# Attention with a routed mixture of experts: the late routing and scatters of batch 5 stand behind head pair 28, and GpSimd drains its DMA queue once ahead of the last 256 rows

## The chip, the cores and the metric

The kernel runs on one core of a Trainium2 chip. The metric is the device time of one execution in microseconds (us); of several runs the median counts. One execution was recorded by the hardware profiler, and all rows below are from that one. The engines are TensorE (PE), VectorE (DVE), ScalarE (ACT), GpSimd (POOL) and SyncE (SP); transfers are issued by an engine's queue and carried by 16 DMA engines.

## The reference

Eight batches of eight heads, 576 positions, head size 64. Attention with rotated q and k, and behind it a mixture of eight experts in which each of the 4,608 tokens goes to the one expert with the largest logit. Cut to what matters:

```python
def _attn_ref(q, k, v):                       # (8, 8, 576, 64)
    q_rot, k_rot = rotate(q), rotate(k)
    scores = scale * q_rot @ k_rot.T
    attn = exp(scores - max) / sum
    return attn @ v

x = attn_out.transpose(0, 2, 1, 3).reshape(4608, 512)

def _moe_ref(x, modality_id, w_gate, modality_bias, w1, w2):
    logits = x @ w_gate + modality_bias[modality_id]      # 8 experts
    e_idx = np.argmax(logits, axis=1)
    gate_w = softmax(logits)[arange(N), e_idx]
    for e in range(8):
        mask = e_idx == e
        h = np.maximum(x[mask] @ w1[e], 0.0)              # 512 -> 1024
        out[mask] = gate_w[mask, None] * (h @ w2[e])      # 1024 -> 512
    return out
```

## The kernel before, in words

The attention works through 32 pairs of heads, n = 0 to 31; four pairs make one batch, so batch 4 ends with pair 19, batch 5 with pair 23, batch 6 with pair 27. For a pair the rope (lines 461 to 469 on POOL) rotates q and k in `ST` and splits them into a high and a low part `HL`; ACT makes the high part at line 452, and a swap (line 477, four transfers on SP's queue) writes `SW`, which is `HL` with its halves exchanged. PE forms the scores (line 492) from `HL` and `SW`, DVE takes the extremes (line 501), ACT the exponentials (line 510), PE turns them round (line 515) and multiplies with v (line 573). DVE and ACT copy between these steps (lines 548 and 452).

When a batch's last pair is done, its rows go to a table `X` in DRAM (lines 633 and 635, SP's queue), and the batch is routed in fifteen steps, `RK0` to `RK14`: logits and their maximum on DVE, the one-hot rows on POOL (`RK6`, lines 687 to 689), the ranks of the tokens within their expert on PE (`RK8`, lines 701 and 703, into a half of a PSUM tile), the running counts `RUN` on DVE (`RK9`, lines 709 and 710), a guard on ACT (`RK10`), the token's own rank on POOL (`RK11`, line 718), the gate on DVE (`RK12`, line 721, into `VAL`), the row number on DVE (`RK13`, line 724) and its cast to a whole number on POOL (`RK14`, line 728). `VO` then writes `VAL` (token id and gate) into the last two columns of `X` (lines 640 and 641). `BKj` loads the j-th 128 tokens of the batch from `X` into one of two buffers `XL`, which alternate in the order of the calls (lines 756 and, for the last 64 tokens, 758), and `SCj` scatters them with an indirect transfer on POOL's queue into the expert's part of a table `XS` (line 738).

The mixture begins while the attention still runs: a first plan uses the rows of batches 0 to 4 in `XS`. A block reads rows of `XS` (lines 1007 and 1030), DVE transposes them, PE multiplies with the first and the second weights (lines 1084, 1202 and 1103, 1326), and POOL scatters the finished rows to the output (line 1114). The weights come in by transfers of SP (line 1034). Behind the blocks of 512 rows a function `chain` does the last planned 256 rows (two stores, line 1114) and a block of 128 rows (two stores, line 1427). A branch for further blocks follows, which is not taken with these inputs (line 1647).

All of this is in an order written out by hand. Each step is put in a list with a key, `EDGE[n].get(name, KEYS[name]) + PER * n` with `PER` = 14.438, and the list is sorted by it. PE, ACT, DVE, POOL and SP each carry out their instructions in that order. `EDGE[19]` are thus the exceptions for the steps of batch 4, `EDGE[23]` those of batch 5. Behind the list the blocks of the mixture are called one after the other.

Of the kernel before, what the change touches and what calls it, by code (L numbers as in the profile page):

```python
# [19 lines left out]
B, H, S, D = 8, 8, 576, 64  # L20
# [110 lines left out]
        "LD1": -42.214,  # L131
    },
    19: {
    },
    23: {
    },
    25: {
        "RE": 11.575, "F2": 13.246, "A_F2": 14.351, "B_F2": 14.486, "RI": 16.427, "AVB": 18.725, "OTB": 20.519, "OUT": 26.426,
# [92 lines left out]
def tile_attention_moe(ctx: ExitStack, tc: tile.TileContext, qk, v, mod, wg, mb, w1, w2, rope, cf, ci, out):  # L231
    nc = tc.nc
# [405 lines left out]
    def vout(b, eng=nc.sync):  # L638
        xd = X[b * S:(b + 1) * S, DM:XU]
        eng.dma_start(out=xd[0:512, :].rearrange("(p j) w -> p j w", j=4), in_=VAL[:, b, 0:4, :].bitcast(F32))  # L640
        eng.dma_start(out=xd[512:576, :], in_=VAL[0:64, b, 4, :].bitcast(F32))
# [93 lines left out]
    def scatter(b, j):  # L735
        oi = bt_[b]["oi"]
        n = P if j < 4 else 64
        inst = nc.gpsimd.indirect_dma_start(  # L738
            out=XS, out_offset=bass.IndirectOffsetOnAxis(ap=oi[0:n, j:j + 1], axis=0),
            in_=xl[b, j][0:n], in_offset=None, bounds_check=E * RS - 1, oob_is_err=False).ins  # L740

        for _b, x in placed:
            tc.declare_no_dep(inst, x, reason="rows of other tokens")
        placed.append((b, inst))
        if b >= NPL:
            for x in taken:
                tc.declare_no_dep(inst, x, reason="the first plan's blocks lie before the rows of later batches")
# [4 lines left out]
    def back(b, j, eng=nc.sync):  # L752
        t = xl[b, j] = XL[len(xl) % 2]
        xd = X[b * S:(b + 1) * S, 0:XU]
        if j < 4:
            eng.dma_start(out=t[:, 0:XU], in_=xd[0:512, :].rearrange("(p j) w -> j p w", j=4)[j])
        else:
            eng.dma_start(out=t[0:64, 0:XU], in_=xd[512:576, :])

    def pads():  # L760
        nc.vector.tensor_copy(CNT, RUN[0:1, B, :])
        for e in range(E):
            r = nc.sync.value_load(CNT[0:1, e:e + 1], min_val=0, max_val=E * RS - BLK)
            inst = nc.sync.dma_start(out=XS[bass.ds(r, BLK), 0:XU], in_=ZR[:, :]).ins
            for _b, x in placed:
                tc.declare_no_dep(inst, x, reason="rows behind those of the tokens")
            for x in taken:
                tc.declare_no_dep(inst, x, reason="the first plan's blocks are full")
            placed.append((B, inst))
# [224 lines left out]
    def m_plan(s):  # L994
        ph, i = slots[s]
        pl = PLB if ph else PLA
        ms[s] = dict(
            e=nc.sync.value_load(pl[0:1, 0, i:i + 1], min_val=0, max_val=E - 1),
            r=nc.sync.value_load(pl[0:1, 1, i:i + 1], min_val=0, max_val=E * RS),
            c=nc.sync.value_load(pl[0:1, 2, i:i + 1], min_val=0, max_val=1))  # L1000

    def m_ix(s):
        d = ms[s]
        k = nt[s]
        ix = d["ix"] = ixp.tile([P, 4, 2], I32, name="ix", tag="ix")
        tab = XS[bass.ds(d["r"], k * P), DM:XU].rearrange("(q a g) w -> g q a w", a=k, g=4)
        m_taken(s, nc.sync.dma_start(out=ix[:, 0:k, :].bitcast(F32), in_=tab).ins)
# [12 lines left out]
    def m_rows(s, j=0):  # L1020
        d = ms[s]
        n = 4 * nt[s]
        if n == 4:
            ho = d["ho"] = ixp.tile([P, 2], I32, name="ho", tag="ho", bufs=1)
            for h in range(2):
                nc.gpsimd.tensor_scalar(ho[:, h:h + 1], d["ix"][:, 0, 0:1], 2.0, float(h), op0=ALU.mult, op1=ALU.add)
        rows = XS[bass.ds(d["r"], nt[s] * P), 0:DM].rearrange("(q r) (i f) -> i q r f", r=n, i=4)[:, :, 8 * j:8 * j + min(n, 8)]
        x = rows_of(s, j).rearrange("p t g f -> p (t g) f")[:, 0:min(n, 8)]
        for i in range(4):
            m_taken(s, nc.sync.dma_start(out=x[32 * i:32 * i + 32], in_=rows[i]).ins)  # L1030
# [26 lines left out]
    def m_split(i, g):  # L1057
        m_hi(i, g)
        m_lo(i, g)

    def m_tr(s, t, j=0):
        x = rows_of(s, j)[:, t]
        nc.vector.transpose(x, x)

    def m_tre(s, t, part=None):
        x = rows_of(s)[:, t].rearrange("p g (c q) -> p c g q", q=32)
        oh, ol = (a[:, :, t * P:(t + 1) * P].rearrange("p c (g q) -> p c g q", q=32) for a in (XTH, XTL))
        if part != 1:
            acopy(oh, x)
        if part != 0:  # L1070
            sub(ol, x, oh.bitcast(F32))
# [390 lines left out]
    def J(k_, nm, n, f, *a):  # L1462
        jobs.append((k_ + PER * n, len(jobs), f, a))
# [30 lines left out]
    for n in range(NPAIR):  # L1494
        def K_(nm, f, *a):
            J(EDGE.get(n, {}).get(nm, KEYS[nm]), nm, n, f, *a)

        for u in range(9):
            K_(f"S{u}", scores, n, u)
            K_(f"MN{u}", rowmin, n, u)  # L1500
            K_(f"EX{u}", expo, n, u)
        for f in ("F0", "F1", "F2", "F3", "FA", "FB"):
            K_(f, fill, n, f)
            for g in range(2):
                K_(f"{'AB'[g]}_{f}", evac, n, f, g)
        for w in range(2):
            c = "AB"[w]
            K_(f"AV{c}", AV, n, w)
            K_(f"OT{c}", avout, n, w)
            K_(f"EV{c}", ev, n, 1 - w)  # L1510
        K_("OUT", outp, n)
        for w in range(2):
            K_("R" + "EI"[w], rsum, n, w)
        if n > 0:
            for part, nm in ((1, "T1"), (0, "T2"), (2, "R"), (3, "HI"), (4, "LO")):
                K_(nm, rope_, n, part)
            for i in range(2):
                K_("SW" + "HL"[i], swap, n, i)
        K_("LV", loadv, n)
        if n > 2:  # L1520
            K_("LD1", load, n, 1)
            K_("LD", load, n, 0)
        if n % 4 == 3:
            K_("BIAS", bias, n // 4)
            K_("XO", xout, n // 4)
            steps = [(f,) for f in route(n // 4)]
            scats = [(scatter, n // 4, j) for j in range(5)]
            if n == z:

                planned = plan()  # L1530
                steps[0:2] = [(each, lambda f: f(), *steps[0:2])]
                late = steps + [(lambda: [vout(B - 1, nc.gpsimd)] + [(back(B - 1, j, nc.gpsimd), scatter(B - 1, j)) for j in range(5)] + [pads()],)] + [(each, next) + ((planned, None),) * 4] * 13
                continue
            for i, x in enumerate(steps):
                K_(f"RK{i}", *x)
            eng = nc.sync if n // 4 < B - 2 else nc.gpsimd
            K_("VO", vout, n // 4, eng)
            for i, x in enumerate(scats):
                K_(f"BK{i}", back, n // 4, i, eng)
                K_(f"SC{i}", *x)  # L1540
# [49 lines left out]
    def chain(lo, hi, begun):  # L1590
        if not begun:
            for g in range(4):
                m_split(0, g)
            for t in range(2):
                m_tr(lo, t)
                m_tre(lo, t)
        for s in range(lo, hi):
            nxt = s + 1 < hi
            half = nt[s] == 1
            if nxt:  # L1600
                if s + 2 < hi:
                    m_rows(s + 2)
                if s + 3 < hi:
                    m_plan(s + 3)
                    m_ix(s + 3)
                for g in range(4):
                    m_load1(s + 1, g)
            if half:
                m_half(s)
            else:  # L1610
                for g in range(4):
                    m_split(1, g)
                    m_l1(s, g)
                    m_l1e(s, g)
            if nxt:
                for g in range(2):
                    m_split(0, g)
                for t in halves(s + 1):
                    m_tr(s + 1, t)
                for t in halves(s + 1):  # L1620
                    m_tre(s + 1, t)
                for g in range(4):
                    m_load2(s + 1, g)
            last = nxt and nt[s + 1] == 1
            if not half:
                m_l2(s, 0)
            if last:
                for g in (2, 3):
                    m_split(0, g)
            if not half:  # L1630
                m_l2(s, 1)
            if nxt and not last:
                for g in (2, 3):
                    m_split(0, g)
# [6 lines left out]
    for s in range(2, NA + NSB):  # L1641
        m_super(s, s + 1)
    assert not late and next(planned, 0) == 0
    chain(NA + NSB, ns, True)
    order.close()
    tot = nc.values_load(TOT[0:1, 0:1], min_val=0, max_val=NB_MAX)
# [103 lines left out]
```

## Time and profile before

| | us |
|---|---|
| median of three runs | 882.19 |
| the three runs | 881.38, 882.19, 886.98 |
| the profiled execution, whole | 884.29 |
| its span on the core | 882.5 |
| busy in it: PE, DVE, ACT, POOL | 833.9, 708.9, 612.2, 453.5 |

The granted TensorE clock was 0.99 of full speed on the mean. The span is the time from the first to the last record of the core; the profiled execution took 1.8 us more than it. A timeline row gives start, duration, engine, line, operation and the names written and read; in brackets stands how long the engine was idle before and what ended that. An engine name with a q behind it (POOLq, SPq) is the engine's sequencer, which carries out semaphores, drains and DMA issues.

### The profile page before, as it was taken

How to read it: one execution, taken by the hardware profiler on the slowest of the kernel's cores; microseconds unless marked ns; L12 is line 12 of the kernel's file. 1: busy time of each engine (PE TensorE's matmuls, PEld its weight loads, DVE VectorE, ACT ScalarE, POOL GpSimd, SP SyncE). 2: the span in 40 equal slices, each digit the busy share in tenths (PEclk: the TensorE clock that was granted, in tenths of full speed). 3: DMA queues.
4: the chain of work that ended last, by engine and by line, in shares of the span. 5: the costliest groups of instructions: out<-in, count | busy, mean ns of one | idle time of the engine just before them, and what ended most of it. 6: DMA issues, size and time to landing. Idle time of an engine off the chain costs nothing.

```text
span 882.5 us, 24889 instructions
## 1 busy us (share of the span) xinstructions
PE 833.9 (94%) x9528; PEld 688.7 (78%) x9528; DVE 708.9 (80%) x1595; ACT 612.2 (69%) x1311; POOL 453.5 (51%) x365
## 2 busy tenths in 40 slices
PE   2899999999999999888999999999999999999992
PEld 2677777777777777676778989898989898989882
DVE  6888898888898888777888577989898998979360
ACT  2898989889888888777975446464656474748360
POOL 2999979989899898999511211024201112020100
PEclk9999999999999999999999999999999999999996
DMA  8877868979788797875877961377955413530520
GB/s 262 229 231 193 260 169 259 265 211 283 205 262 245 215 279 205 249 213 171 251 213 187 328 181 49 60 219 224 282 139 186 114 38 88 169 101 8 186 73 14
DMA packets 116330, 165.80 MB, mean 188 GB/s; under 512 B 31180, under 2 KB 76894, under 8 KB 116204
## 3 DMA queue, kind: packets, MB, share of 16 engines
q1 hardware_dynamic: 107468, 139.18, 55.2%
q0 software_dynamic: 7392, 23.34, 7.5%
q8 instruction: 77, 1.26, 0.6%
q10 hardware_dynamic: 1344, 1.62, 0.6%
q14 instruction: 49, 0.40, 0.1%
HBM read 118.14 MB, written 34.70 MB: 173 GB/s over the span
## 4 chain that ended last, share of the span: by engine, by line
PE 79%; DMA 5%; POOL 4%; ACT 4%; DVE 3%; issue 2%; SPq 1%; ACTq 0%; POOLq 0%; DVEq 0%
PE psY L1326 20%; PE ps L573 15%; PE psH L1202 14%; PE ps L492 13%; PE ps L515 9%; PE ps L608 2%; DMA SW<-HL 2%; PE psY L1202 2%; ACT P L510 1%; PE psH L1084 1%; PE psY L1103 1%; DMA ST<-in_rope_dram 1%; POOL HL L469 1%; DVE sc L501 1%; DMA ST<-in_moe_w_dram 1%
## 5 line engine op out<-in xcount | busy, mean ns | idle before, releaser
L501 DVE CUSTOM_DVE_ANT_1 sc<-ps,ZERO 128x576 f32<-128x576 f32 x288 | 206.6, 748 | 24.0 <-PE ps L492 11.3
L510 ACT ACTIVATE P<-sc,mn 128x576 f32<-128x576 f32 x256 | 195.5, 767 | 5.9 <-DVE mn L501 4.7
L492 PE MATMUL ps<-HL 64*128 64x288 f32 x960 | 167.9, 309 | 13.7 <-ACT HL L452 10.8
L492 PE MATMUL ps<-SW 64*128 64x288 f32 x960 | 168.1, 309 | 7.6 <-DMA SW<-HL 7.5
L1114 POOL DMA_INDIRECT out_dram<-sc,ix x36 | 43.4, 1206 | 222.1 <-ACT sc L1113 215.4
L492 PEld LDWEIGHTS ps<-HL 64*128 64x128 f32 x960 | 134.4, 188 | 19.5 <-ACT HL L452 10.8
L492 PEld LDWEIGHTS ps<-SW 64*128 64x128 f32 x960 | 134.3, 188 | 11.9 <-issue 9.4
L573 PE MATMUL ps<-PH,AT 128*64 128x320 f32 (+1 forms) x1024 | 139.6, 415 | 4.0 <-DVE PH L548 3.7
L1202 PE MATMUL psH<-HL,W1H 128*128 128x256 f32 x600 | 126.4, 279 | 0.4 <-ACT HL L452 0.4
L1202 PE MATMUL psH<-HL,W1L 128*128 128x256 f32 x400 | 111.6, 279 | 0.0
L573 PEld LDWEIGHTS ps<-PH,AT 128*64 128x64 f32 x1024 | 68.4, 137 | 53.1 <-DVE PH L548 7.0
L548 DVE COPY PH<-ps 128x512 f32<-128x512 f32 (+1 forms) x160 | 98.3, 630 | 11.0 <-PE ps L515 8.8
L452 ACT ACTIVATE PH<-ps 128x512 f32<-128x512 f32 (+1 forms) x160 | 85.3, 551 | 29.6 <-PE ps L515 26.0
L515 PEld LDWEIGHTS ps<-idf,P 64*128 64x128 f32 x2304 | 86.0, 138 | 20.7 <-ACT P L510 8.5
L1326 PE MATMUL psY<-W2L,SW 128*128 128x512 f32 x256 | 101.3, 396 | 0.0
L1326 PE MATMUL psY<-W2H,SW 128*128 128x512 f32 x256 | 100.9, 394 | 0.0
L515 PE MATMUL ps<-idf,P 64*128 64x64 f32 x2304 | 97.3, 225 | 2.8 <-ACT AT L452 1.7
L1202 PEld LDWEIGHTS psH<-HL,W1H 128*128 128x128 f32 x600 | 98.8, 188 | 1.1 <-ACT HL L452 0.6
L469 POOL TENSOR_TENSOR HL<-ST,HL 128x1152 fp32r<-128x1152 f32 x31 | 82.5, 2660 | 24.4 <-ACT HL L452 24.3
L465 POOL TENSOR_TENSOR ST<-ST 128x1152 f32<-128x1152 f32 x30 | 79.5, 2651 | 1.1
L738 POOL DMA_INDIRECT XS<-XL,oi x40 | 44.8, 1120 | 66.1 <-DMA XL<-X 45.2
L1202 PEld LDWEIGHTS psH<-HL,W1L 128*128 128x128 f32 x400 | 75.2, 188 | 0.0
(286 smaller groups left out, 1829.6 us busy)
## 6 DMA issues: line engine op xcount, KB each, us to landing
ST<-in_moe_w_dram SPq DMA_DIRECT2D x88, 512.0 KB
ST<-in_qk_dram SPq DMA_DIRECT2D x62, 576.0 KB
SW<-HL SPq DMA_DIRECT2D x124, 216.0 KB
AT<-in_v_dram SPq DMA_DIRECT2D x32, 256.0 KB
X<-X SPq DMA_DIRECT2D x8, 1024.0 KB
XL<-X SPq DMA_DIRECT2D x24, 257.0 KB
XG<-XS SPq DMA_DIRECT2D x40, 128.0 KB
XS<-ZR SPq DMA_DIRECT2D x8, 514.0 KB
```

The source lines that it names most:

```text
L452: return nc.scalar.activation(o, i, AF.Copy, scale=scale)
L465: e.tensor_tensor(a, a, b, op=ALU.add)
L469: e.tensor_tensor(d["HL"][:, 1, o], a, d["HL"][:, 0, o].bitcast(F32), op=ALU.subtract)
L492: nc.tensor.matmul(ps[:, g, 0:288], t[:, wq, q0:q0 + P], t[:, wk, k0:k0 + 288], start=(m == 0), stop=(m == len(L) - 1))
L501: nc.vector.tensor_tensor_reduce(sc, d.pop(("S", u))[:, :, 0:288], ZERO.unsqueeze(2).to_broadcast([P, 2, 288]), 1.0, FMAX, ALU.add, ALU.mi ...
L510: nc.scalar.activation(p, sc.rearrange("p a b -> p (a b)"), AF.Exp, bias=mn, scale=-1.0, accum_out=d["sum"][:, u:u + 1])
L515: nc.tensor.transpose(ps[:, g, c:c + 64], src[r, k0:k0 + P], idf[r, r])
L548: alone(d["at", f], g, (nc.vector.tensor_copy if g else acopy)(o, i).ins, int(f[1] in "23B"))
L573: i = nc.tensor.matmul(pa[hh * 64:hh * 64 + 64, 0:c1 - c0], d["V"][:, hh, kt, :], r, start=(kt == 0), stop=(kt == 4))
L738: inst = nc.gpsimd.indirect_dma_start(out=XS, out_offset=bass.IndirectOffsetOnAxis(ap=oi[0:n, j:j + 1], axis=0), in_=xl[b, j][0:n], in_off ...
L1202: nc.tensor.matmul(ps[b][:, r * BLK:r * BLK + BLK], w[:, c, f0:f0 + P], x[:, c, :], start=(first and r == 0 and c == 0 and i == 0), stop=( ...
L1326: nc.tensor.matmul(po[t], hx[:, c, o:o + P], w[:, c, :], start=(k == 0 and c == 2 * q and i == 0), stop=(k == 3 and c == 2 * q + 1 and i = ...
```

## The change

It has three parts. The keys of some steps of batch 4 and batch 5 change; batch 5's `VO` and `BK` go to POOL's queue instead of SP's; and one `drain` is called on POOL ahead of `chain`.

```diff
     19: {
+        "BK0": 71.4, "BK1": 71.5, "BK3": 95.0, "BK2": 116.0, "BK4": 131.0,
+        "SC3": 113.825, "SC2": 128.215, "SC4": 152.075,
     },
     23: {
+        "VO": 129.3, "BK3": 130.0, "BK4": 130.1, "BK2": 132.5, "BK1": 133.0, "BK0": 137.0,
+        "RK6": 45.016, "RK7": 49.391, "RK8": 52.824, "RK9": 58.16, "RK10": 79.988, "RK11": 109.721, "RK12": 128.347, "RK13": 128.956,
+        "RK14": 129.684, "SC3": 130.859, "SC4": 132.359, "SC2": 132.942, "SC1": 136.961, "SC0": 137.506,
     },
@@
-            eng = nc.sync if n // 4 < B - 2 else nc.gpsimd
+            eng = nc.sync if n // 4 < B - 3 else nc.gpsimd
             K_("VO", vout, n // 4, eng)
@@
     assert not late and next(planned, 0) == 0
+    nc.gpsimd.drain()
     chain(NA + NSB, ns, True)
```

Five lines more stand ahead of the functions, so line 701 of before is line 706 of the changed kernel, and so on. The drain adds one instruction to POOL; it stands between the four stores of the last 512-row block and the two stores of the 256 rows.

On PE the ranks of batch 5 move. Before, they stand behind the last products of line 492 and the turning of `P_120`, among the work of two later pairs (`ps_126` to `ps_129` are the halves of the PSUM tiles):

```order
L492 MATMUL ps_126<-HL_87 128x288
L492 MATMUL ps_126<-SW_89 128x288
L515 MATMUL ps_129<-idf,P_120 128x64 x16
L701 LDWEIGHTS UT
L701 MATMUL ps_127<-OH,UT 128x48
...
L608 MATMUL ps_128<-RW,AT 64x72 x18
L515 MATMUL ps_126<-idf,P_119 128x64 x16
L573 MATMUL ps_127<-PH_124,AT 64x256 x8
```

In the changed kernel, at the same place:

```order
L497 MATMUL ps_128<-SW_89 128x288
L706 LDWEIGHTS UT
L706 MATMUL ps_127<-OH,UT 128x48
...
L497 MATMUL ps_126<-HL_87 128x288
...
L520 MATMUL ps_129<-idf,P_120 128x64 x16
L613 MATMUL ps_128<-RW,AT 64x72 x18
L520 MATMUL ps_126<-idf,P_119 128x64 x16
L578 MATMUL ps_129<-PH_124,AT 64x256 x8
```

The ranks went ahead of the last six products into `ps_126` and of the turning into `ps_129`, and the product with v (line 573, now 578) writes `ps_129` instead of `ps_127`.

On SP two loads of batch 5 stood around the writes of `X` and ahead of the last pair's swap (`XL_82` and `XL_83` are the two buffers, `in_v_dram` is v):

```order
L756 DMA XL_83<-X 128x514
L1034 ISA
L1034 DMA ST_74<-in_moe_w_dram 128x4x256
L633 DMA X<-X 512x1x512
L635 DMA X<-XT 64x8x32 x2
L353 DMA AT<-in_v_dram 128x2x256
L356 DMA AT<-in_v_dram 64x64 x2
L756 DMA XL_82<-X 128x514
L477 DMA SW_89<-HL_87 64x864 x4
```

The changed kernel has there:

```order
L1039 ISA
L1039 DMA ST_74<-in_moe_w_dram 128x4x256
L638 DMA X<-X 512x1x512
L640 DMA X<-XT 64x8x32 x2
L358 DMA AT<-in_v_dram 128x2x256
L361 DMA AT<-in_v_dram 64x64 x2
L482 DMA SW_89<-HL_87 64x864 x4
```

The loads are gone from this queue; the rest is as before.

On POOL, behind the last rope, before (the scatter at the top is the last one of batch 5, what follows is batch 6):

```order
L738 DMA XS<-XL_83,oi 39424x528
L718 TENSOR_TENSOR rk<-rk,OH 128x40
L640 DMA X<-VAL 512x1x2
L641 DMA X<-VAL 64x2
L728 CAST oi<-of 128x5
L756 DMA XL_82<-X 128x514
L756 DMA XL_83<-X 128x514
```

In the changed kernel the whole row of batch 5 stands here, ahead of batch 6's:

```order
L645 DMA X<-VAL 512x1x2
L646 DMA X<-VAL 64x2
L723 TENSOR_TENSOR rk<-rk,OH 128x40
L733 CAST oi<-of 128x5
L761 DMA XL_83<-X 128x514
L763 DMA XL_82<-X 64x514
L743 DMA XS<-XL_83,oi 39424x528
L743 DMA XS<-XL_82,oi 39424x528
L761 DMA XL_83<-X 128x514
L743 DMA XS<-XL_83,oi 39424x528
L761 DMA XL_82<-X 128x514
```

Seven transfers came to POOL's queue (two writes of `VAL`, five loads), and five scatters moved to the end of the attention. With them batch 5's cast and first scatter left their place between two rope steps, and the last three scatters of batch 4 stand later between such steps than before.

## Rows read from the trace of the kernel before

**Rows 1.** The page: busy us, share of the span, instructions of each engine
```profile
PE 833.9 (94%) x9528; PEld 688.7 (78%) x9528; DVE 708.9 (80%) x1595; ACT 612.2 (69%) x1311; POOL 453.5 (51%) x365
```
**Rows 2.** Chain of waits, its last piece: start us, us, what
```profile
867.66 0.45 POOL out_dram L1427
```
**Rows 3.** Records of line 1746: operation xcount, duration ns min/median/max, first and last start
```profile
L1746 POOLq DRAIN  x3: 46/109/8241, 873.4 to 882.2; - x3
L1746 SPq DRAIN  x3: 7/7/13, 874.1 to 881.9; - x3
```
**Rows 4.** Records of line 1746 from 873 to 874 us
```profile
L1746 POOLq DRAIN  x1: 8241/8241/8241, 873.4 to 873.4; - x1
```
**Rows 5.** Groups by line on POOL: xcount | busy us, mean ns | idle before, releasers
```profile
L738 POOL DMA_INDIRECT XS<-XL,oi x40 | 44.8, 1120 | 66.1 <-DMA XL<-X 45.2 <-DVE oi L728 15.3 <-issue 5.3
L1114 POOL DMA_INDIRECT out_dram<-sc,ix x36 | 43.4, 1206 | 222.1 <-ACT sc L1113 215.4 <-issue 5.2 <-ACT AT L452 1.2
...
L756 POOL DMA_DIRECT2D XL<-X x8 | 4.6, 580 | 11.8 <-DMA XS<-XL,oi 10.2 <-DMA X<-VAL 1.1 <-issue 0.4
```
**Rows 6.** Timeline of POOL, 826 to 869 us: start, us, what [idle before <-releaser]
```profile
831.51 0.98 POOL L1114 DMA_INDIRECT out_dram<-sc,ix  x1 [0.41 <-ACT sc L1113]
848.35 0.98 POOL L1114 DMA_INDIRECT out_dram<-sc,ix  x1 [15.86 <-ACT sc L1113]
```
**Rows 7.** Records of line 1114: from issue to landing
```profile
DMA to landing us min/median/max: 4.0/4.6/6.9
```
**Rows 8.** Timeline of PE, 386 to 392 us
```profile
387.12 0.40 PE L492 MATMUL ps<-HL 64*128 64x288 f32 x1 [0.87 <-ACT AT L452]
...
389.36 0.20 PE L701 MATMUL ps<-OH,UT 128*128 128x48 bf16 x1 [1.08 <-DVE PH L548]
389.40 0.27 PE L703 MATMUL ps<-OH,ON 128*128 128x40 bf16 x5
...
391.44 0.87 PE L573 MATMUL ps<-PH,AT 128*64 128x256 f32 x6 [0.34 <-DVE RUN L710]
```
**Rows 9.** Timeline of DVE, 388.5 to 392 us
```profile
391.31 1.27 DVE L548 COPY PH<-ps 128x512 f32<-128x512 f32 x2
```
**Rows 10.** Timeline of POOL, 394 to 413 us
```profile
410.71 0.18 POOL L728 CAST oi<-of 128x5 int32<-128x5 f32 x1
411.18 1.10 POOL L738 DMA_INDIRECT XS<-XL,oi  x1 [0.29 <-POOL oi L728]
```
**Rows 11.** Waits of PE, 380 to 420 us: us in total, times, longest
```profile
PE ps L515 <- ACT AT L452: 1.7, 1, 1.7
```
**Rows 12.** Waits of PE, 420 to 470 us
```profile
PE ps L492 <- DMA SW<-HL: 1.5, 1, 1.5
```
**Rows 13.** Timeline of SP's queue, 426 to 442 us
```profile
435.14 0.54 SPq L756 DMA_DIRECT2D XL<-X  x1
435.77 4.55 SPq L477 DMA_DIRECT2D SW<-HL  x4
```
**Rows 14.** Timeline of SP's queue, 402 to 408 us
```profile
403.56 2.42 SPq L477 DMA_DIRECT2D SW<-HL  x4
```
**Rows 15.** Windows: length, busy us of PE, PEld, DVE, ACT, POOL, clock, DMA share, GB/s
```profile
460.00:480.00 20.00, 20.00 (x220) 17.09 (x213) 17.21 (x32) 11.38 (x20) 1.42 (x2) 1.00 0.81 205
495.00:502.00 7.00, 6.29 (x53) 5.89 (x51) 4.43 (x7) 3.49 (x6) 0.59 (x1) 1.00 1.03 373
502.00:845.00 343.00, 342.51 (x2156) 307.24 (x2157) 282.86 (x405) 196.09 (x285) 57.16 (x51) 1.00 0.47 140
```
**Rows 16.** Chain of waits, 480 to 503 us
```profile
489.92 5.84 DMA ST<-in_moe_w_dram
```
**Rows 17.** Timeline of POOL, 455 to 535 us
```profile
481.09 1.15 POOL L756 DMA_DIRECT2D XL<-X  x2 [0.44 <-issue]
...
512.54 0.93 POOL L738 DMA_INDIRECT XS<-XL,oi  x1 [0.94 <-DMA XL<-X]
...
532.50 1.42 POOL L1114 DMA_INDIRECT out_dram<-sc,ix  x1 [17.74 <-ACT sc L1113]
```

## The prediction, made before the changed kernel was run

> **What bounds the kernel now.** I began with the busy times on the page: TensorE (PE) works 833.9 of 882.5 us [rows 1]. While PE runs without a gap, no other engine can change the time. So two kinds of place matter: those where PE waits, and the end, where PE has no more to do. I took the end from the chain of waits and the records of the closing line, the stretch out of which work moves (380 to 460 us) from PE's waits and the timelines, and the stretch into which it moves (464 to 502 us) from the table of windows.
>
> The last store of the output leaves the GpSimd engine (POOL) at 867.7 us, and that is POOL's last work [rows 2]. The rest is closing: at 873.4 POOL begins a DRAIN of 8.24 us [rows 4]. The other two drains of POOL on that line take 46 and 109 ns [rows 3]. So a single drain is the longest thing in the last 15 us, and it waits for no computing.
>
> **The drain in front of the last 256 rows.** What do the 8.24 us pay for? The short drains come with no transfer issued since the drain before; the long one is the first behind all of POOL's transfers. The three groups that hold most of these are 40 scatters, 36 stores and 8 loads, 84 in all [rows 5]; 8.24 us over 84 is at most 98 ns each. I read it as work per transfer since the last drain, an estimate from one duration. The change's drain stands between the four stores of the last 512-row block and the next two; these two and the two of the last 128 rows remain behind it: 4 x 98 ns = 0.4 us for the final drain.
>
> That does not give back all of 7.8 us, because SP is late next: its last drains run from 874.1 [rows 3]. POOL's long one ends near 881.7, and the handshake after it would begin at about 874.2 instead: 881.7 - 874.2 = 7.5 us.
>
> What does the new drain cost? POOL's fourth store ends at 832.5 and it then waits for ScalarE (ACT) until 848.35 [rows 6], 15.9 us. A store lands at most 6.9 us after its issue [rows 7]; if the drain waits for that and then works 8.3 us, and 0.7 us more for the seven transfers that the change adds to POOL, it is over at 831.5 + 6.9 + 9.0 = 847.4. Queued behind it are only the store at 848.35 and three more. Nothing reads what they write, and late by a few us the first two would still go out ahead of the last at 867.7. I cost the place at nothing. Bounds of this term: 0 (the price doesn't go with the number) and -7.5.
>
> **Batch 5's ranks, earlier on PE.** PE waits 1.08 us in front of the ranks, for a copy on VectorE (DVE) that frees their PSUM half, and 0.34 us in front of line 573, for the running counts behind them [rows 8]. The ranks last from 389.36 to 389.67. In the changed order they stand ahead of the last six products of line 492, where PE waits 0.87 us for ACT (up to 387.12): they fit into that gap, and both waits, 1.42 us, go. But line 573 now takes the other half and waits for one DVE copy, 0.64 us (two take 1.27 [rows 9]): -1.42 + 0.64 = -0.8; bounds 0 and -1.4.
>
> At 410.7 POOL runs batch 5's cast, 0.18 us, and after 0.29 us its first scatter, between two rope steps [rows 10]. Both leave this place; a scatter of batch 4 comes in one step earlier. PE's wait for ACT behind that rope is 1.7 us [rows 11]. 0.47 us less some 0.17 us that a scatter's issue costs anyway: -0.3; bounds 0 and -0.5.
>
> **Batch 5's loads leave SP's queue.** The load at 435.1, 0.54 us, stands just ahead of the four swap transfers of the last head pair, whose issues take 4.55 us [rows 13]; four at 403.6 took 2.42 [rows 14]. PE waits 1.5 us for that swap, its only wait between 420 and 470 [rows 12]. The 0.54 us go surely and up to 2.1 us of slow issue may; the wait caps it. I take -1.2, since ACT's half of the input was ready only at the same time as SP; bounds 0 and -1.5.
>
> PE stands still for 0.5 us between 502 and 845 [rows 15], so what is won before stays won. By the same token SP's other waits in batch 5, which end there without PE waiting, are given nothing.
>
> **Batch 5's rows move to 464 to 490 us.** Five loads and five scatters of up to 128 x 514 numbers of 4 bytes (263 KB, the last half) are 2.4 MB. They leave 400 to 456 us and come behind VAL, on POOL's queue. Two buffers alternate, and each load waits for a scatter to land; batch 6's chain of that kind runs from 481.1 to 513.5 [rows 17]. Batch 5's fills about 464 to 490 and pushes batch 6's some 9 us later, to 522; POOL has nothing to do before its store at 532.5, which covers that. The transfer engines are full near there: share 1.03 at 373 GB/s from 495 to 502, and PE loses 0.7 of those 7 us, the most in the table [rows 15]. The chain of waits runs over a transfer of the second weights, 5.84 us, that ends at 495.8 [rows 16]. Batch 6's rows going out of that stretch balance most of batch 5's coming in; 0.3 MB are left over, an estimate, at 373 GB/s: +0.8. Bounds: 0, and all 2.4 MB ahead of that load at the 205 GB/s which the engines moved from 460 to 480 [rows 15]: +11.7.
>
> **Sum.** -7.5 - 0.8 - 0.3 - 1.2 + 0.8 = -9.0 us. The profiled execution took 884.29 (a span of 882.5 and 1.8 around it), 2.1 above the median of 882.19. So 875.3 for it and 873.2 on the median. With the small terms at their good ends it is 871.3, and with those at zero and 2 us of contention 877.
>
> **A rule that speaks against it.** The Trainium skill, "PSUM — Partial Sum Buffer", section "Engine vs sequencer instructions", says that a drain waits for the engine to go fully idle. By it alone the drain at 873.4 would be short, POOL having been idle since 868, the new one would take nothing off it, and the sum would be -1.5. The trace disagrees: 8.24 us on an idle engine.
>
> **Rivals.**
> *The final drain keeps its time.* If 8.24 us is the price of a DRAIN behind any transfer, whatever their number, the four late stores bring it back, and only the routing's -0.8 - 0.3 - 1.2 + 0.8 = -1.5 remains: 880.7 (879.5 to 882.5). For it: a single such duration is in the trace, so nothing shows it grow. Against it: 8.24 us is odd as a fixed price beside 46 and 109 ns.
> *The moved rows delay the second weights.* If all 2.4 MB go ahead of the load that ends at 495.8, at 205 GB/s, PE waits 11.7 us longer there, not 0.8: 873.2 + 10.9 = 884.1. It turns the total slower from 9.8 us on, that is below 2.4 MB / 9.8 us = 245 GB/s. For it: 205 and 373 GB/s both stand in the table, the former already at a share of 0.81. Against it: the rows are paced by each other's landings, and at 373 GB/s it would cost 6.4, leaving 878.8. The Trainium skill, "DMA: Bandwidth & Descriptors", section "Issuing engines are not separate DMA queues", says that transfers issued by SP and GpSimd run on the same engines and interleave; the share of 1.03 with both at work fits that.
> *The routing's gains are covered.* Then -7.5 alone: 874.7, inside the first case.
>
> **Chances.** Final drain short, small gains: 0.76. Final drain stays: 0.17. The moved rows eat the gain: 0.07. The first case has its own range, 871.3 to 877; the range given takes in the second, up to 882.5, and goes down to 869.5 for waits that I costed at nothing. One per cent, about what a measurement of this kernel can tell from no change, is 8.8 us, so faster means under 873.4. My value stands at that edge: of the first case 0.45 is faster and 0.31 the same; the second (0.17) and 0.03 of the third are the same, too, 0.04 slower.
>
> **What would show it.** At the end: POOL's last DRAIN near 0.4 us, SP's closing work last, and a new DRAIN of 8 to 15 us behind the store at 831. If the last one is still 8 us, the reading per transfer is wrong. At 387 to 391: the wait of 1.08 gone; at 416: below 1.5; at 441: the wait for the swap near 0.3. From 495 to 502: if PE loses well over 0.7 us, or the load of the second weights takes well over 6, the moved rows cost more than I allow. A time above 878 would mean that the drain or the moved rows were mis-sized; one below 870 that waits I called covered were not.

## The result, and the profile after

The changed kernel took 872.34 us, the median of six runs (868.67 to 875.68), against 881.98 for the kernel before in the same session: 0.9869 of it, with a 95% interval of 0.9824 to 0.9915. The prediction was 873.2, within 869.5 to 882.5. Its profiled execution took 873.96 us (span 872.1); that of before had taken 884.29, so the two traces below are 10.3 us apart.

Where these went can be read from two places. The last store leaves POOL 1.5 us earlier than in [rows 2], and behind it the closing stretch is 872.1 - 866.1 = 6.0 us in place of 882.5 - 867.7 = 14.8. So 8.8 of the 10.3 us lie behind the last store. The chain of waits after, its last piece (start us, us, what):

```profile
866.12 0.45 POOL out_dram L1432
```

The records of the closing lines after, and of the new drain (operation xcount, duration ns min/median/max, first and last start); they answer to [rows 3, 4]:

```profile
L1653 POOLq INC_SWDGE_SEM  x1: 280/280/280, 870.2 to 870.2; - x1
L1752 POOLq DRAIN  x3: 46/109/380, 870.5 to 871.8; - x3
L1752 SPq DRAIN  x3: 7/7/13, 871.2 to 871.5; - x3
L1649 POOLq DRAIN  x1: 7129/7129/7129, 829.8 to 829.8; - x1
```

The long drain is now 0.38 us. The new one takes 7.1 us at 829.8, where POOL's next store comes only at 846.8. One thing happened ahead of it: in front of the second store of that block POOL stood idle for 1.85 us, where it had stood 0.38 in before. The experiments below come back to this. Timeline of POOL, before and then after:

```profile
828.71 0.98 POOL L1114 DMA_INDIRECT out_dram<-sc,ix  x1 [0.38 <-ACT sc L1113]
```
```profile
828.66 0.99 POOL L1119 DMA_INDIRECT out_dram<-sc,ix  x1 [1.85 <-ACT sc L1118]
```

Before the long drain at the end there is one more instruction that the prediction left out of its sum. In the trace of before it took 2.2 us:

```profile
L1647 POOLq INC_SWDGE_SEM  x1: 2200/2200/2200, 871.2 to 871.2; - x1
```

On PE the waits of [rows 8, 11] and [rows 12] became these from 380 to 420 us (us in total, times, longest); from 420 to 470 us PE waits for nothing:

```profile
PE ps L520 <- ACT AT L457: 1.6, 1, 1.6
PE ps L520 <- ACT P L515: 0.4, 1, 0.4
PE ps L520 <- issue: 0.3, 1, 0.3
```

The ranks stand at 385.9 with no wait, and the product with v that waited for them starts 2.1 us earlier than in [rows 8]; the products ahead of them started 0.3 us earlier already (384.5 against 384.8). Timeline of PE after, 385 to 390 us:

```profile
385.91 0.20 PE L706 MATMUL ps<-OH,UT 128*128 128x48 bf16 x1
...
389.36 0.87 PE L578 MATMUL ps<-PH,AT 128*64 128x256 f32 x6
```

SP issues the last pair's swap at once (timeline of SP's queue after, answering to [rows 13]), with no load ahead of it:

```profile
431.17 2.47 SPq L482 DMA_DIRECT2D SW<-HL  x4
```

Two places got worse. Batch 5's rows run through POOL's queue from 460 to 498 us, 38 us and not 26, and batch 6's last scatter goes out at 531.2, not near 522. Timeline of POOL after, answering to [rows 17]:

```profile
460.17 0.62 POOL L761 DMA_DIRECT2D XL<-X  x1 [0.24 <-DMA X<-VAL]
...
498.48 0.81 POOL L645 DMA_DIRECT2D X<-VAL  x1
...
505.02 1.13 POOL L761 DMA_DIRECT2D XL<-X  x2 [4.97 <-issue]
...
531.16 0.92 POOL L743 DMA_INDIRECT XS<-XL,oi  x1 [0.42 <-issue]
532.38 0.98 POOL L1119 DMA_INDIRECT out_dram<-sc,ix  x1 [0.30 <-issue]
```

The store at 532.4 is the second of the first block, which left at 513.8 before. The rows behind it were the surprise: ScalarE waits for that store's buffer (waits of ACT, 500 to 552 us), and PE in the end for the one-hot rows of the last batch (waits of PE, 505 to 600 us), where it had waited 0.5 us before (the last line):

```profile
ACT sc L1118 <- DMA out_dram<-sc,ix: 3.4, 1, 3.4
```
```profile
PE psY L706 <- DVE OH L694: 2.2, 1, 2.2
```
```profile
PE psY L701 <- DVE OH L689: 0.5, 1, 0.5
```

From 495 to 502 us PE lost 1.0 us where it had lost 0.7 [rows 15], and the load of the second weights took 6.83 us where it had taken 5.84 [rows 16] (a window and a piece of the chain, after):

```profile
495.00:502.00 7.00, 6.01 (x50) 5.61 (x49) 6.30 (x10) 4.02 (x6) 2.57 (x4) 1.00 1.09 363
```
```profile
485.70 6.83 DMA ST<-in_moe_w_dram
```

These 0.3 us lie within what traces differ by: from 480 to 510 us PE stands idle for 0.3 to 1.8 us in the nine traces with batch 5's loads on SP's queue (before and the experiments below), and for 0.3 to 1.6 us in the five with the loads moved.

### The profile page after: what moved, and what is told of

Same layout as the page of the kernel before. It is cut to its first block, busy times and chain, and to the rows that moved or that the text cites. A ratio compares the mean times of both kernels' runs of the same rounds, so it can differ in the third digit from the quotient of the medians.

```text
span 872.1 us, 24882 instructions
## 1 busy us (share of the span) xinstructions
PE 835.3 (96%) x9528; PEld 690.2 (79%) x9528; DVE 709.2 (81%) x1595; ACT 611.8 (70%) x1311; POOL 463.2 (53%) x372
## 4 chain that ended last, share of the span: by engine, by line
PE 79%; DMA 5%; POOL 5%; DVE 4%; issue 3%; ACT 2%; SPq 1%; POOLq 0%; ACTq 0%; DVEq 0%
PE psY L1331 21%; PE ps L578 15%; PE psH L1207 14%; PE ps L497 12%; PE ps L520 9%; PE ps L613 2%; DMA SW<-HL 2%; PE psY L1207 2%; PE psH L1089 1%; PE psY L1108 1%; POOL HL L474 1%; DMA X<-VAL 1%; ACT P L515 1%; DMA ST<-in_moe_w_dram 1%; PE ps L1089 1%
## 5 line engine op out<-in xcount | busy, mean ns | idle before, releaser
L497 PE MATMUL ps<-HL 64*128 64x288 f32 x960 | 170.6, 311 | 13.1 <-ACT HL L457 10.9
L743 POOL DMA_INDIRECT XS<-XL,oi x40 | 48.5, 1213 | 77.3 <-DMA XL<-X 56.6
```

The lines of the kernel that those rows point to most:

```text
L497: nc.tensor.matmul(ps[:, g, 0:288], t[:, wq, q0:q0 + P], t[:, wk, k0:k0 + 288], start=(m == 0), stop=(m == len(L) - 1))
L743: inst = nc.gpsimd.indirect_dma_start(out=XS, out_offset=bass.IndirectOffsetOnAxis(ap=oi[0:n, j:j + 1], axis=0), in_=xl[b, j][0:n], in_off ...
```

## The experiments

**The two parts apart.** First the drain alone:

```diff
     assert not late and next(planned, 0) == 0
+    nc.gpsimd.drain()
     chain(NA + NSB, ns, True)
```

> The kernel before with the one GpSimd drain and no moved step. Theory of the prediction, with what the changed kernel's profile showed (last DRAIN 0.38 us, the semaphore instruction ahead of it 0.28 us in place of 2.20): the closing stretch from the last store (867.7 in before) to the end shrinks from 14.8 us to about 6.0, so some 8.8 us less, about 873.2 on the median; the prediction's own term was 7.5 us, 874.7. Rival (the price of the last drain does not go with the number of transfers): no change, 882. Nothing of PE's waits between 380 and 560 us may differ from before by more than a few tenths.

Measured: 873.36 us against 883.57 in its session, 0.9888 (0.9858 to 0.9918). The last store leaves at 865.5, the span ends at 871.4: a closing stretch of 5.9 us, as expected. PE's waits between 380 and 470 us are of the same kinds as in before, among them 1.2 us ahead of the ranks and 1.5 for the swap. Two got shorter although nothing was changed there: 0.3 us for 0.9 at 385 us, and none for the 1.1 us for a copy at 398 us. The last store left 2.2 us earlier than in before without any move, which is more than the 1.5 us of the changed kernel.

Then the moves alone, the changed kernel without that line:

> The changed kernel without its drain: only the moved steps. The moves should give what the last store's time shows, 1.5 us earlier than before (866.1 against 867.7), so about 880.5 on the median, and POOL's last DRAIN over 8 us again with 107 transfers. If the two parts do not simply add, this run is above 882 (moves lose by themselves) or below 878.

Measured: 872.09 us, 0.9863 (0.9834 to 0.9891), some 8 us less than I expected. So each half of the change brings nearly all of the gain, and the two do not add up. The trace shows how. With the moves alone and no drain ahead of the end, the closing instructions are short too:

```profile
L1652 POOLq INC_SWDGE_SEM  x1: 476/476/476, 868.8 to 868.8; - x1
L1751 POOLq DRAIN  x3: 46/109/1217, 869.3 to 871.1; - x3
```

POOL issued 107 transfers in this run and none was drained before, yet the last DRAIN takes 1.2 us and not the 8.8 that 107 transfers would cost.

**What the last drain pays for.** One drain in the middle, behind the fifth block:

```diff
     for s in range(2, NA + NSB):
         m_super(s, s + 1)
+        if s == 4:
+            nc.gpsimd.drain()
```

> The kernel before with one drain behind the fifth block only, so that some 16 to 24 stores remain behind it in place of 4. By transfers: the last DRAIN takes 70 to 98 ns for each, 1.2 to 2.3 us, and the semaphore instruction ahead of it some 0.5 us. Fixed price: over 7 us. Only the first drain is slow, whenever it comes: about 0.4 us.

876.69 us (where no interval is given, here and below, the time is that of one execution), against 883.57 for the kernel before; POOL's closing instructions:

```profile
L1649 POOLq INC_SWDGE_SEM  x1: 596/596/596, 871.7 to 871.7; - x1
L1748 POOLq DRAIN  x3: 46/109/1687, 872.3 to 874.5; - x3
```

The drain in the middle began at 664.1, and four stores of its block left between 661.7 and 667.8, inside it or just before; 20 transfers are left behind these. 4 transfers gave 380 ns, 20 give 1687: 82 ns for each.

Drains behind every block:

```diff
+    nc.gpsimd.drain()
     for s in range(2, NA + NSB):
         m_super(s, s + 1)
+        nc.gpsimd.drain()
```

> The kernel before with a drain behind the second block, behind every 512-row block after it and so ahead of the last 256 rows too. If the price goes with the transfers since the last drain: the first of these drains takes 4 to 6 us (some 60 transfers), those behind four or eight stores each under 1 us of work beside the wait for their landings, the last one 0.4. If a drain behind any transfer has a fixed price, each takes 7 to 8 us.

The closing drain is 375 ns, as with one drain. The eight inner ones take 3.5 to 12.2 us, but their rows begin before the stores ahead of them have left, so they hold waiting for ScalarE and for landings as well; this run does not tell work from waiting, and the expectation of under 1 us of work behind four stores cannot be read from it. It took 872.16 us, so one execution gives no sign that eight drains at such places cost anything.

**What shortened the drain without a drain.** The moves add seven transfers to POOL's queue. So seven others, which nothing reads, were added to the kernel before, at 512 us:

```diff
+    DUM = cst.tile([P, 16], F32, name="DUM")
@@
     m_l2(0, 1)
+    for i in range(7):
+        nc.gpsimd.dma_start(out=DUM[0:128, 2 * i:2 * i + 2], in_=cf[0:128, 0:2])
     for g in range(4):
```

> The kernel before, no drain and no moved step, with seven extra small loads (128 partitions x 8 bytes, read by nothing) on GpSimd's queue behind the second store, at about 514 us: 107 transfers in place of 100, as with the moves. Theory: what shortened the closing DRAIN in the moves alone is their seven more transfers (something frees the queue's entries before the end once about a hundred have been issued), so here too the last DRAIN is 1 to 2 us and the semaphore instruction ahead of it some 0.5. Rival (it is where the moved transfers stand, not how many there are): 8.2 to 9 us and 2.2 us or more.

873.71 us against 880.22, with no drain and no move:

```profile
L1650 POOLq INC_SWDGE_SEM  x1: 436/436/436, 869.2 to 869.2; - x1
L1749 POOLq DRAIN  x3: 46/109/1054, 869.7 to 871.3; - x3
```

So it is the additional transfers. The same with one partition in place of 128:

> As the run with seven extra loads, but each of them loads 8 bytes into a single partition. If transfers are counted: the same last DRAIN as there. If what is counted is the rows or pieces of a transfer: seven pieces in place of 896 are too few, and the last DRAIN stays at about 8.3 us.

884.12 us, no gain at all:

```profile
L1650 POOLq INC_SWDGE_SEM  x1: 2336/2336/2336, 870.1 to 870.1; - x1
L1749 POOLq DRAIN  x3: 46/109/8812, 872.5 to 881.8; - x3
```

Seven transfers more than before, 8812 - 8241 = 571 ns more, 82 ns for each again. And three of 128 partitions, and one:

> Three extra loads of 128 partitions in place of seven: 103 transfers. If the queue's entries are freed at a threshold between 100 and 103, the last DRAIN is short, about 0.3 us shorter than with seven by the 73 ns for each transfer behind it; if the threshold lies higher, it is longer than before, about 8.5 us.

> One extra load of 128 partitions in place of three, no drain and no moves: 101 transfers. With three and seven the queue's entries were freed and 8 and 12 transfers were left for the last DRAIN (0.73 and 1.05 us; 82 ns each). If the threshold lies just above the kernel before, one is enough and the last DRAIN takes under 0.7 us; if two or three are needed, it takes 8.2 + 0.1 = 8.3 us.

873.66 us with three, 882.78 with one. The closing instructions of both:

```profile
L1650 POOLq INC_SWDGE_SEM  x1: 356/356/356, 869.9 to 869.9; - x1
L1749 POOLq DRAIN  x3: 46/109/727, 870.3 to 871.6; - x3
```
```profile
L1650 POOLq INC_SWDGE_SEM  x1: 2216/2216/2216, 869.5 to 869.5; - x1
L1749 POOLq DRAIN  x3: 46/109/8322, 871.8 to 880.6; - x3
```

With 100, 101 and 107 transfers that nothing cleared, the last DRAIN takes 8241, 8322 and 8812 ns: it goes with their number at 82 ns, and so does the semaphore instruction, at some 19. Three or seven transfers with 128 rows, but neither one with 128 nor seven with one, make the kernel clear what has piled up: 727 and 1054 ns are the price of 8 and 12 transfers, and the 1217 ns of the moves alone that of 14.

The traces point to where it was cleared. In each of these kernels there is one late store, ahead of which POOL stands idle for longer than the 0.4 us of before: the seventh from the end in the moves alone (as in the changed kernel), the fifth from the end with seven loads, the last one with three. Timeline of POOL in the three runs:

```profile
827.89 0.99 POOL L1119 DMA_INDIRECT out_dram<-sc,ix  x1 [1.85 <-ACT sc L1118]
```
```profile
830.81 1.28 POOL L1115 DMA_INDIRECT out_dram<-sc,ix  x1 [1.93 <-ACT W2H L453]
```
```profile
867.00 0.99 POOL L1428 DMA_INDIRECT out_dram<-sc,ho  x1 [2.78 <-ACTq L1650]
```

With one load, and with seven of one partition, no store is late. From the late store on 7, 5 and 1 transfers go out, and the last DRAIN pays for 14, 12 and 8: for these and seven more each time. The late store comes 1.5 to 2.3 us later than the 0.4 us would have it.

What is counted fits rows. A store has 128. With three loads the limit is met at the last store, with 384 rows more than the kernel before issues in all. With seven loads (896 rows) it is met four stores, 512 rows, earlier: 384 again. The seven moved transfers have 512 + 64 rows of `VAL` and 4 x 128 + 64 of loads, 1152, and it is met six stores, 768 rows, earlier than with three: 384 again. In each run the store before passed, with 256. So by this reckoning from the kernel's shapes the limit lies between 256 and 384 rows above what the kernel before issues. The number of transfers does not fit: the late store is the 103rd of POOL's transfers with three and with seven loads, but the 101st with the moves, and 107 passed with the small loads. Nor do bytes fit: the moved loads have up to 263 KB each, the added ones 1 KB. What the queue holds in all, and why seven stay behind, is open.

So in the changed kernel the queue was cleared before the new drain began, and by this reckoning that drain found 10 transfers. It took 7.1 us all the same, with two stores leaving inside it; in the drain alone, where 96 had piled up, it took 9.1 us.

**The ranks alone.** The drain, and of the moves only `RK6` to `RK9` of batch 5:

```diff
     23: {
+        "RK6": 45.016, "RK7": 49.391, "RK8": 52.824, "RK9": 58.16,
     },
@@
+    nc.gpsimd.drain()
     chain(NA + NSB, ns, True)
```

> The kernel before with the drain, and of the moves only batch 5's one-hot, sums, ranks and running counts earlier (RK6 to RK9). If the ranks' place is what took PE's waits away between 385 and 400 us in the changed kernel (3.4 us of waits before, 0.4 after), they are gone here too and the wait of 1.5 us for the last pair's swap at about 440 stays; no wait before the last batch's ranks at 547 beyond the 0.5 us of the drain alone. On the median 1.5 to 3 us less than the drain alone, 870.5 to 872. Rival (batch 4's moves or the free SP queue took them away): the waits at 386 stay, and the time is that of the drain alone, 873.4.

872.73 us, 0.9906 (0.9876 to 0.9936), inside the interval of the drain alone: on the clock no gain is shown. PE's waits from 380 to 420 us:

```profile
PE ps L516 <- ACT AT L453: 2.2, 1, 2.2
PE ps L493 <- DMA SW<-HL: 1.0, 3, 0.6
```

The 1.2 us ahead of the ranks and both waits of 0.3 beside them are gone, by the ranks' place alone; a swap of another pair now makes PE wait 1.0 us. The wait for the last pair's swap shrank to 0.3 here, against what I expected. That wait is not a steady one: in the eight traces whose instructions are the same up to there (before, the drain alone, the drains behind every block and in the middle, and the four runs with additional loads) it is 1.5, 1.5, 0.9, 0, 1.3, 2.3, 1.1 and 0 us, 1.1 on the mean. So the 0.3 here says nothing of the ranks.

**Everything but the ranks.** The changed kernel with `RK6` to `RK10` at their old keys:

```diff
-        "RK6": 45.016, "RK7": 49.391, "RK8": 52.824, "RK9": 58.16, "RK10": 79.988, "RK11": 109.721, "RK12": 128.347, "RK13": 128.956,
+        "RK11": 109.721, "RK12": 128.347, "RK13": 128.956,
```

> The changed kernel with batch 5's one-hot, sums, ranks and counts back at their old keys (RK6 to RK10); the loads stay on GpSimd's queue, the drain stays. Theory: PE's waits before and behind the ranks (0.3 + 1.2 + 0.3 us with the drain alone) return, and the wait of 1.5 us for the last pair's swap stays away, since it is the loads' place on SP's queue that held the swap up; some 1.5 to 2 us slower than the change, 870.5 to 874. Rival (the swap's wait went because the ranks moved, as in the run with the ranks alone): it is back at 1.3 to 1.5 us.

874.67 us against 884.76, 0.9889 (0.9859 to 0.9920). From 420 to 470 us PE waits for nothing, as in all five traces with the loads off SP's queue. That speaks for the loads' place as the cause of the swap's wait, though two of the eight other traces are at 0 too. The ranks' waits are back; and the last batch's one-hot rows keep PE waiting at 547. Waits of PE, 380 to 420 and 500 to 600 us:

```profile
PE ps L706 <- DVE PH L553: 1.2, 1, 1.2
...
PE ps L497 <- ACT AT L457: 0.3, 1, 0.3
PE ps L578 <- DVE RUN L715: 0.3, 1, 0.3
```
```profile
PE psY L706 <- DVE OH L694: 1.6, 1, 1.6
```

What the loads' move wins at the swap, 1.1 us on the mean, it gives back there (1.6 in place of 0.5).

**The late store.** If the second store of the first block is what ScalarE waits for, it should be called ahead of batch 6's rows:

```diff
     J(end + 0.1, "moe", z, m_l2, 0, 0)
+    J(end + 0.11, "moe", z, m_l2, 0, 1)
@@
-    m_l2(0, 1)
     for g in range(4):
```

> The changed kernel with the second store of the first block called right behind the first, ahead of batch 6's remaining rows on GpSimd's queue (the order of PE's products is the same). Theory: in the changed kernel that store went out at 532.4 in place of 513.8, so ScalarE waited 3.4 us at 535 for its buffer, and PE 2.2 us at 546 for the one-hot rows of the last batch. Here ScalarE's wait is gone and PE's wait at 547 is 0.5 us as without the moves: 1.7 us less, about 870.6 against 872.3 of the change. Rival (the pushed-back rows of batch 6 themselves, not the store's buffer, hold the last batch up): PE's wait at 547 stays at 1 to 2 us.

> The changed kernel once more, beside the run with the earlier store: about 872 on the median, PE's wait before the last batch's ranks 1 to 2.2 us again (1.1 in the moves alone).

865.79 us (0.9840, 0.9816 to 0.9864) with the earlier store, 868.88 us (0.9854, 0.9830 to 0.9878) for the change beside it. The second store now leaves at 499.6, right behind the first (timeline of POOL), and ScalarE no longer waits for a store; in the change beside it the wait is still there (waits of ACT, 500 to 552 us):

```profile
498.22 1.04 POOL L1119 DMA_INDIRECT out_dram<-sc,ix  x1 [0.30 <-issue]
499.57 1.02 POOL L1119 DMA_INDIRECT out_dram<-sc,ix  x1 [0.30 <-issue]
```
```profile
ACT sc L1118 <- DMA out_dram<-sc,ix: 2.6, 1, 2.6
```

But PE's wait at 547 is 0.5 us in both of these traces: a wait of 2.6 us on ACT still fits in front of it, one of 2.9 to 3.4 does not. So the cause of ScalarE's wait is shown, and the 3.1 us between the two medians are not: their intervals overlap. It is the fastest kernel measured here.

## Why the prediction was right, and where it was not

The total came out as forecast, 872.3 against 873.2, and the step that carried it holds: the last DRAIN goes with the transfers since the last clearing, at 82 ns (the forecast had at most 98, from one duration), and the place for a new drain at 830 us costs nothing; the drain alone shows both. The rival of a fixed price is ruled out by the 1687 to 8812 ns for 20, 100, 101 and 107 transfers. That the total fits so closely is in part luck: the end brought more than forecast, and the same kernel measured again gave 868.9. By the rule that a drain waits for the engine to go fully idle (the Trainium skill, "PSUM — Partial Sum Buffer", section "Engine vs sequencer instructions"), taken alone, all four would have been short; the rows disagree.

**The size of that term**: 8.8 us and not 7.5. The DRAIN itself gave back 7.9 us, and the semaphore instruction ahead of it 1.9 more (2.2 to 0.28), which the prediction left out; waiting for the last landing took 0.5 us longer, and what follows the DRAIN 0.3. SP was late next, as the prediction said: its drain at 871.2 stands behind the end of POOL's at 870.9. But the prediction took 874.1 for a time of SP's own. It comes 0.7 us behind the start of POOL's DRAIN in before and does so after (871.2 and 870.5), so both stand behind the semaphore instruction. The prediction saw POOL at work at 873.4 and did not ask what had held it there.

**Whose gain it is**: the prediction gave it to the drain and would have expected 880.7 without it. The moves alone gave 872.1, since with seven more transfers POOL's queue is cleared on the way, at the seventh store from the end. The step "and 0.7 us more for the seven transfers that the change adds" is the one that failed: they were counted as a cost of the drain, and nothing in the trace of before could show that they remove it. In the changed kernel either half would have been enough: its closing stretch is 6.0 us, that of the moves alone 5.9 (871.3 - 865.4).

**The ranks**, -0.8: the size fits, the terms do not. The waits for ACT, for the copy and for the running counts between 385 and 391 us went, 1.8 us in the trace of everything but the ranks (0.3, 1.2 and 0.3), and line 573 did not wait for a copy as I had put in their place. But with the whole change PE waits elsewhere, 0.4 to 0.9 us for the exponentials at 395 to 401. An estimate of what is left: from 385 to 420 us PE stands idle for 3.3 us with the ranks alone and 4.2 on the mean of the eight traces without a move, and for 2.5 in the four with all moves and 3.9 without the ranks: 0.8 to 1.4 us. **The cast**, -0.3: PE's wait for ACT stayed at 1.6 us; nothing. **The swap**, -1.2: 1.1 on the mean of eight traces, from 0 to 2.3; that all five with the loads moved are at 0 speaks for the reason given. **The moved rows**, +0.8: no run shows this cost; the 0.3 us from 495 to 502 are inside what the traces differ by.

**What was missed** is the cover: "POOL has nothing to do before its store at 532.5" was true of before, but the chain ended at 532.1 and not at 522, and a store of the first block stood behind it, for whose buffer ScalarE had to wait. It cost PE 0.6 to 1.7 us more than in before in three of the four runs with the moved loads and the late store, and nothing in the fourth. What the moves as a whole bring beside the closing stretch is not shown. On the clock the change is at 0.9869 and 0.9854, the drain alone at 0.9888, and their intervals overlap; the 1.5 us by which the last store left earlier are no measure, since the drain alone gave 2.2. An estimate from the traces: from 385 to 560 us PE stands idle for 4.3 to 5.7 us in three with all moves (4.8 on the mean) and for 4.8 to 8.4 in the eight with none (6.5), so 1.7 us, near the forecast's 1.5.

## What to carry to other kernels

Look at the end of the trace behind the last store: a long DRAIN there on GpSimd is paid for each transfer of its own queue that has piled up, and a drain at a place where GpSimd waits anyway takes it off the end. (SP issued 541 transfers in before, and its closing drains took 7 to 13 ns.) Measure the halves of a change apart; two parts can have one gain. Read a small wait in several traces before you give it a price: the swap's was 0 to 2.3 us with the same instructions. When a chain of transfers is moved onto a queue, list every instruction that comes to stand behind it, and reckon its rounds from the busy stretch it moves into.

## What the runs showed of the hardware

Seven transfers of 8 bytes from 128 partitions each, which nothing reads, made the kernel some 6.5 us faster (873.7 against 880.2); seven from one partition made it no faster (884.1). Each of the two is a single execution; the DRAIN and the semaphore instruction ahead of it account for 9.7 of the 10.4 us between them.

Two profiles can differ by several us where the instructions are the same: the first store of the last block leaves at 827.3 us in before and at 825.1 in the drain alone, ahead of the only difference between them, and the last store at 866.1 and 862.8 in the two traces of the changed kernel. One part of that is TensorE's clock, which falls to 0.50 of full speed, 1.2 GHz, for some us. In before it was low at 364 to 366 us, behind a wait of PE of 2.6 us that ended at 363.7; after, PE waited 2.4 us at the same place and the clock stayed at 1.00, but it was low at 414 to 416 us, behind a wait of 1.6 us. Windows of before, then of after (the last but two is the clock):

```profile
364.00:366.00 2.00, 2.00 (x10) 0.80 (x10) 1.70 (x6) 1.62 (x4) 1.83 (x2) 0.50 0.95 259
414.00:416.00 2.00, 0.85 (x12) 0.64 (x10) 1.32 (x6) 1.01 (x1) 2.00 (x2) 1.00 0.05 17
```
```profile
364.00:366.00 2.00, 1.35 (x10) 0.77 (x12) 2.00 (x6) 0.70 (x2) 2.00 (x1) 1.00 1.02 357
414.00:416.00 2.00, 2.00 (x34) 2.00 (x34) 1.81 (x3) 1.74 (x5) 2.00 (x2) 0.50 0.77 209
```

So a term of 1 or 2 us is read from its own wait, in more than one trace, and not from the time of a single execution.
